# The last half of a down projection summed on 128 partitions of 64 columns instead of 32 partitions of 256

## The chip, the cores and the metric

The kernel runs on one core of one Trainium2 chip. The metric is the device time of one execution in microseconds (us); three runs of the kernel before took 438.18, 437.98 and 438.04, median 438.04. The core has five engines that run their own instruction streams and wait for each other by semaphores: PE (TensorE, the matrix array, with its weight loads shown apart as PEld), DVE (VectorE), ACT (ScalarE), POOL (GpSimd) and SP (SyncE, which here only issues transfers). Sixteen transfer engines move data between memory (HBM) and the on-chip SBUF. TensorE writes into PSUM, from which VectorE and ScalarE read. SBUF and PSUM have 128 partitions; a matmul loads a stationary operand ("weights" of the array, up to 128 columns wide) and streams a moving operand past it, column by column; the stationary columns become the partitions of the result.

## What is computed

One decoding step of a transformer block for 8 sequences of one token each, width 1024:

```
mod = (silu(c) @ w_mod) in six parts: sa, ca, ga, sb, cb, gb
h = layernorm(x) * (1 + ca) + sa
x = x + ga * attention(h)        # 32 query heads on 4 cached heads, 8192 cached keys and values each
h = layernorm(x) * (1 + cb) + sb
g = h @ W_gate ; u = h @ W_up    # 1024 -> 3584
x = x + gb * ((relu(g) * u) @ W_down)   # 3584 -> 1024
```

Inputs and outputs are bfloat16. The change is in the last line: the product with W_down, the gate gb, the residual, and the store of the result, which is 8 rows of 1024.

## The kernel before

All weights and both caches (185 MB) are read once, by transfers that SP issues in the order of the list `stream` into one large SBUF tile, `ring`, of five slots. A transfer waits for the matmuls that used what lay in its place before. Instructions are written out in program order for each engine; a small graph (`_Graph`, lines 36 to 232) turns data dependences into semaphore waits. No planner moves anything.

The first part makes mod, the normalised input and the queries. The middle loop goes over 16 pairs of cached heads and is followed by the output projection. The last part, which the change touches, goes like this:

- Lines 691 to 697: the attention result becomes `x1T`, the residual stream with the width on partitions (128 x 8 x 8), and is normalised to `h2T`.
- Lines 700 to 709: 128 matmuls for gate and up, in eight steps of k. After step 3 stand two calls of `to_rows` (line 540). `to_rows` brings gb and `x1T` from the width-on-partitions form into the form in which the result will be made: VectorE multiplies the source by the mask `part` into the tile `wide` (f32, eight blocks of 128 columns), TensorE multiplies each block of `wide` by the mask `rest`, and VectorE copies the result out of PSUM into `gbR` or `x1R`. In this kernel the form is 32 partitions of interest (partition 32 q + b, for quarter q of the width and sequence b) of 256 columns each.
- Lines 710 to 716: relu and product, `hmR`; seven transposes and a copy make `hmT`, the stationary operand of the down projection: 128 partitions, 7 x 4 blocks of 8 columns (one column for each sequence).
- Lines 719 to 723: the first half of W_down, block ("wd", 0), 28 matmuls of 8 weight columns by 512, into four strips of partitions of the PSUM bank `Y`. Line 724 copies it to `yR`.
- Lines 725 and 726, the fold: two f32 matmuls with the selection matrix `fold` add up the four strips of `yR` and lay the sum out as 256 columns on the 32 partitions, in the PSUM tile `W`. In the profile an f32 matmul shows as two records.
- Lines 727 to 736: the second half of W_down, blocks ("wd", 1) to ("wd", 4), 56 matmuls of 8 weight columns by 256, four at a time side by side: quarter q of the width into the strip of partitions that begins at 32 q. They add to the fold's result in PSUM.
- Lines 737 and 738: VectorE multiplies by `gbR` into `fR` and adds `x1R` into `outR`.
- Lines 739 to 741: four stores, one for each quarter, of eight pieces of 512 bytes; two issued on SP, two on ACT. Line 755 waits for all four.

The masks and cleared tiles (`part`, `rest`, `wide`, `fold`, lines 460 to 466) are made at the start, on VectorE.

In the profile the helper lines stand for all operations: line 422 is every matmul, 426 every transpose, 430 every VectorE operation, 433 every ScalarE operation, 747 every load, 87 every other transfer.

Of the kernel before, what the change touches and what calls it, by code (L numbers as in the profile page):

```python
# [7 lines left out]
ALU = mybir.AluOpType  # L8
AX = mybir.AxisListType
# [225 lines left out]
def bass_adaLN_cond__gqa_block_cached__glu_gated_reglu__decode_kernel(  # L235
# [14 lines left out]
    B, _, D = A_x.shape  # L250
# [7 lines left out]
    KD = D // 128  # L258
# [7 lines left out]
    g = _Graph()  # L266
    f32, bf16 = dt.float32, dt.bfloat16

    with ExitStack() as es:
        E = es.enter_context  # L270

        def sb(name, shape, dtype):
            return E(nc.sbuf_tensor(name, shape, dtype))
# [5 lines left out]
        identf = sb("identf", [128, 128], f32)  # L279
# [8 lines left out]
        yR = sb("yR", [128, 512], f32)  # L288
# [12 lines left out]
        ov = sb("ov", [128, 256], f32)  # L301
# [6 lines left out]
        diag = sb("diag", [128, 2, 128], bf16)  # L308
        blk = sb("blk", [128, 8, 16], f32)
        pick = sb("pick", [128, 2, B], f32)  # L310
        fold = sb("fold", [128, 2, 128], f32)
        og = sb("og", [128, 2, 16], f32)
        spare = sb("spare", [128, 2, 16], bf16)
        ot = sb("ot", [128, 2, 16, B], bf16)
        hmT = sb("hmT", [128, 7, 4, B], bf16)
        part = sb("part", [128, 4], f32)
        rest = sb("rest", [128, 32], f32)
        wide = sb("wide", [128, KD, 128], f32)
        gbR = sb("gbR", [128, 256], f32)
        x1R = sb("x1R", [128, 256], f32)  # L320
        outR = sb("outR", [128, 256], bf16)
# [5 lines left out]
        fR = ov[:, 0:256]  # L327
# [4 lines left out]
        osem = E(nc.semaphore("d_o"))  # L332
# [46 lines left out]
        wd = B_W_down.rearrange("(q p i) n -> p q i n", q=4, i=7)  # L379
# [13 lines left out]
        for key, at, cols, src, shape, slot in stream:  # L393
# [3 lines left out]
            t = ring[:, lo:hi]  # L397
# [6 lines left out]
            o = _Op("sp", None, 0)  # L404
# [7 lines left out]
        def pe(fn, reads=(), writes=(), block=None, deps=()):  # L412
            deps = list(deps)
            if block is not None:
                deps.append(loads[block])
            o = g.op("pe", fn, reads, writes, deps)
            if block is not None:
                users[block] = o
            return o

        def mm(out_, lhsT, rhs, start, stop, reads, writes, block=None, deps=()):
            return pe(lambda e: e.matmul(out_, lhsT, rhs, start=start, stop=stop, skip_group_check=True),  # L422
                      reads, writes, block, deps)

        def tr(out_, in_, ident, reads, writes, block=None):
            return pe(lambda e: e.matmul(out_, in_, ident, start=True, stop=True, is_transpose=True),  # L426
                      reads, writes, block)

        def dve(name, *args, reads=(), writes=(), **kw):
            return g.op("dve", lambda e: getattr(e, name)(*args, **kw), reads, writes)  # L430
# [29 lines left out]
        dve("tensor_reduce", part[:], identf[:].rearrange("p (q x) -> p q x", q=4), AX.X, ALU.add, reads=["identf"], writes=["part"])  # L460
        dve("tensor_reduce", rest[:], identf[:].rearrange("p (q x) -> p x q", q=4), AX.X, ALU.add, reads=["identf"], writes=["rest"])
        dve("memset", wide[:], 0.0, writes=["wide"])
        dve("memset", fold[:], 0.0, writes=["fold"])
        for i in range(2):
            dve("tensor_reduce", fold[:, i].rearrange("p (h s r) -> p h s r", h=2, s=2)[:, :, i, :],
                identf[:].rearrange("p (a h r) -> p h r a", a=2, h=2), AX.X, ALU.add, reads=["identf", "fold"], writes=["fold"])
        dve("tensor_reduce", pick[:], identf[:].rearrange("p (s h x) -> p h x s", s=2, h=2)[:, :, 0:B, :], AX.X, ALU.add, reads=["identf"], writes=["pick"])
        for i in (0, 1, 2, 3, 7):
            dve("memset", bank(i), 0.0, writes=[pB[i]])
# [37 lines left out]
        for k in range(KD):  # L507
            w = place[("mod", k // 4)][:, k % 4, :]
# [5 lines left out]
        t = PS[:, 4, :]  # L514
# [19 lines left out]
        for j in range(2):  # L534
            dve("tensor_copy", qT[:, :, 16 * j:16 * (j + 1)].rearrange("p b (q i) -> p i q b", i=4),
                TB(0)[:, 0:512].rearrange("p (i q x) -> p i q x", i=4, q=4)[:, :, :, B * j:B * (j + 1)],
                reads=[pT[0], ("KT", 2)], writes=["qT", ("KT", 2)])


        def to_rows(dst, dkey, src, skey):  # L540
            dve("tensor_tensor", out=wide.rearrange("p k (q x) -> p k q x", q=4)[:, :, :, 0:B], in0=src[:, :, None, :].to_broadcast([128, KD, 4, B]),
                in1=part[:, None, :, None].to_broadcast([128, KD, 4, B]), op=ALU.mult, reads=[skey, "part"], writes=["wide"])
            for k in range(KD):
                mm(W[:, 32 * k:32 * (k + 1)], wide[:, k, :], rest[:], True, True, ["wide", "rest"], [pW])
            dve("tensor_copy", dst.rearrange("p (x k) -> p k x", k=8), W[:, 0:256].rearrange("p (k x) -> p k x", k=8), reads=[pW], writes=[dkey])


        turn = [0]
# [90 lines left out]
        Y, pY = bank(0), pB[0]  # L639
# [73 lines left out]

        for i in range(7):
            tr(TB(0)[:, 128 * i:128 * (i + 1)], hmR[:, i:896:7], identb[:], [("KT", 2), "identb"], [pT[0]])
        dve("tensor_copy", hmT[:], TB(0)[:, 0:896].rearrange("p (i q x) -> p i q x", i=7, q=4)[:, :, :, 0:B], reads=[pT[0]], writes=["hmT"])


        for t in range(14):
            w = place[("wd", 0)][:, t // 7, t % 7, :]  # L720
            for h in range(2):
                at = 64 * (t % 2) + 32 * h
                mm(Y[at:at + B, :], hmT[:, t % 7, t // 7, :], w[:, 512 * h:512 * (h + 1)], t < 2, t >= 12, ["hmT"], [pY], ("wd", 0))
        dve("tensor_copy", yR[:], Y, reads=[pY], writes=["yR"])
        for i in range(2):
            mm(W[:, 0:256], fold[:, i], yR[:, 256 * i:256 * (i + 1)], i == 0, False, ["yR", "fold"], [pW])
        for c_ in (2, 3):
            for i in range(7):
                if c_ == 2:
                    key, w = ("wd", 1), place[("wd", 1)][:, i, :]  # L730
                else:
                    u = 2 + (i >= 4) + (i >= 6)
                    key, w = ("wd", u), place[("wd", u)][:, i - (0, 4, 6)[u - 2], :]
                for q in range(4):
                    mm(W[32 * q:32 * q + B, 0:256], hmT[:, i, c_, :], w[:, 256 * q:256 * (q + 1)], False, c_ == 3 and i == 6,
                       ["hmT"], [pW], key)
# [18 lines left out]
        nc.sync.wait_ge(osem, 64)  # L755


# [26 lines left out]
```

## Time and profile before

| what | us |
|---|---|
| median of three runs | 438.04 |
| span of the profiled execution, first to last instruction | 436.3 |
| TensorE busy | 307.2 (70%) |
| ScalarE busy | 208.4 (48%) |
| VectorE busy | 180.0 (41%) |
| GpSimd busy | 12.6 (3%) |
| bytes moved, mean rate | 185.81 MB, 426 GB/s |

The record holds no separate time of the profiled execution; its span is 1.7 us under the median of the runs. The page divides the span into 40 slices of 10.9 us and gives a digit for each (9 is 90% busy or more); PEclk is the share of its full clock that TensorE was granted. The chain of work that ended last is followed back from the last instruction. The timeline gives the start, the duration, the engine, the line, the operation, what it writes and reads, its shapes, how many were merged, and in brackets how long the engine had been idle and what ended that. A table by windows gives, for each stretch, its length, the busy time and count for PE, PEld, DVE, ACT and POOL, then the granted clock, the share of the transfer engines and GB/s.

### The profile page before, as it was taken

What the parts mean: (1) busy time and instruction counts of PE and PEld (TensorE: products, weight loads), DVE (VectorE), ACT (ScalarE), POOL (GpSimd) and SP (SyncE); (2) the same over time, 40 slices, a digit from 0 to 9 for tenths busy, and PEclk for the clock granted to TensorE, in tenths of its full rate; (3) what the DMA queues carried; (4) which work ended last, traced back from release to release, by engine and by line L of the source; (5) the groups of instructions that cost most, each with busy time, mean ns of one, the idle gap of its engine ahead of it and who ended that gap; (6) DMA issues with size and microseconds to landing.
All of it is one profiled execution on the core that took longest, in us unless ns stands there. A gap on an engine that the chain in (4) does not pass through costs nothing.

```text
span 436.3 us, 10723 instructions
## 1 busy us (share of the span) xinstructions
PE 307.2 (70%) x4575; PEld 200.1 (46%) x4575; DVE 180.0 (41%) x384; ACT 208.4 (48%) x246; POOL 12.6 (3%) x52
## 2 busy tenths in 40 slices
PE   0104257989878888787888888777888878755356
PEld 0101025656555555554555555555555555432323
DVE  3600036456363644536264553536364453331111
ACT  2200005676756747675664757576575747400000
POOL 6000000000000000000000000000000000000000
PEclk9999599999999999999999999999999999885766
DMA  8999999999999999999999999999999999999996
GB/s 339 433 433 446 431 431 432 434 431 431 433 436 433 436 433 436 433 436 433 433 436 433 436 436 433 433 436 436 433 436 433 433 433 433 420 422 439 430 419 251
DMA packets 7003, 185.81 MB, mean 426 GB/s; under 512 B 800, under 2 KB 832, under 8 KB 1104
## 3 DMA queue, kind: packets, MB, share of 16 engines
q1 hardware_dynamic: 6928, 185.61, 98.8%
q8 instruction: 9, 0.15, 0.1%
q10 hardware_dynamic: 64, 0.04, 0.0%
q14 instruction: 2, 0.02, 0.0%
HBM read 185.63 MB, written 0.02 MB: 426 GB/s over the span
## 4 chain that ended last, share of the span: by engine, by line
DMA 54%; PE 23%; DVE 9%; issue 8%; ACT 5%; SPq 0%; DVEq 0%; ACTq 0%; POOL 0%
DMA ring<-in_A_k_cache_dram 34%; PE PS L422 13%; DMA ring<-in_w_mod_dram 11%; PE PS L426 11%; DMA ring<-in_B_W_down_dram 8%; ACT P L433 3%; DVE KT L430 2%; ACT KT L433 2%; DVE tm L430 2%; DVE ov L430 1%; DVE nm L430 1%; DVE mp L430 1%; DVE rl L430 0%; DVE nb L430 0%; DVE qT L430 0%
## 5 line engine op out<-in xcount | busy, mean ns | idle before, releaser
L433 ACT ACTIVATE KT<-PS 128x1024 bf16<-128x1024 bf16 (+1 forms) x130 | 131.9, 1016 | 164.2 <-PE PS L426 137.7
L426 PE MATMUL PS<-identb,ring 128*128 128x128 bf16 x2048 | 152.8, 220 | 22.0 <-DMA ring<-in_A_k_cache_dram 20.3
L430 DVE COPY KT<-PS 128x1024 bf16<-128x1024 bf16 (+1 forms) x129 | 88.9, 689 | 164.2 <-PE PS L426 129.1
L426 PEld LDWEIGHTS PS<-identb,ring 128*128 128x128 bf16 x2048 | 117.0, 98 | 61.3 <-issue 36.9
L422 PE MATMUL PS<-KT,Z 128*32 128x512 bf16 x516 | 51.9, 389 | 0.1
L422 PE MATMUL PS<-ring,pt 128*32 128x256 bf16 x1088 | 49.8, 274 | 0.6 <-DVE pt L430 0.6
L433 ACT ACTIVATE P<-PS,nb 64x1024 bf16<-64x1024 f32 x34 | 37.7, 1108 | 6.2 <-DVE nb L430 4.2
L426 PE MATMUL PS<-identb,P 128*128 128x128 bf16 x272 | 21.1, 221 | 20.2 <-ACT P L433 14.5
L422 PEld LDWEIGHTS PS<-ring,pt 128*32 128x32 bf16 x1088 | 24.5, 95 | 12.8 <-issue 0.8
L422 PE MATMUL PS<-ring,siluT 128*24 128x512 bf16 x96 | 8.6, 531 | 27.6 <-DMA ring<-in_w_mod_dram 27.6
L426 PEld LDWEIGHTS PS<-identb,P 128*128 128x128 bf16 x272 | 15.5, 98 | 26.5 <-DVE KT L430 17.2
L433 ACT ACTIVATE pt<-PS 64x512 bf16<-64x512 bf16 x34 | 20.1, 591 | 13.5 <-PE PS L426 13.3
L430 DVE COPY pt<-PS 64x512 bf16<-64x512 bf16 x34 | 14.4, 422 | 17.7 <-PE PS L426 17.2
L430 DVE TENSOR_REDUCE mp<-PS 128x1 f32<-128x1024 f32 x17 | 20.7, 1215 | 0.0
L422 PEld LDWEIGHTS PS<-KT,Z 128*32 128x32 bf16 x516 | 13.3, 92 | 13.8 <-ACT KT L433 0.5
L422 PE MATMUL PS<-ring,h2T 128*8 128x512 bf16 (+1 forms) x128 | 10.5, 494 | 11.7 <-DMA ring<-in_B_W_up_dram 9.8
L433 ACT ACT_TABLE_LOAD x11 | 14.1, 1283 | 8.4 <-DMA KT<-in_A_x_dram 8.3
L422 PEld LDWEIGHTS PS<-ring,siluT 128*24 128x24 bf16 x96 | 2.9, 120 | 33.0 <-DMA ring<-in_w_mod_dram 28.3
L426 PE MATMUL PS<-identb,KT 128*128 128x128 bf16 (+1 forms) x19 | 1.7, 217 | 18.4 <-DVE KT L430 18.4
L637 POOL CAST ot<-og 128x16 bf16<-128x16 f32 x16 | 4.1, 254 | 291.0 <-DVE og L430 291.0
L422 PE MATMUL PS<-od,selo 128*128 128x128 f32 x36 | 8.8, 326 | 5.1 <-DVE od L430 5.1
L422 PEld LDWEIGHTS PS<-ring,h2T 128*8 128x8 bf16 x128 | 3.5, 109 | 18.0 <-DMA ring<-in_B_W_up_dram 11.1
(99 smaller groups left out, 163.3 us busy)
## 6 DMA issues: line engine op xcount, KB each, us to landing
ring<-in_A_k_cache_dram SPq DMA_DIRECT2D x16, 4096.0 KB, 21.6
ring<-in_A_v_cache_dram SPq DMA_DIRECT2D x16, 4096.0 KB, 30.5
ring<-in_w_mod_dram SPq DMA_DIRECT2D x2, 6144.0 KB, 42.5
ring<-in_A_wq_dram SPq DMA_DIRECT2D x2, 4096.0 KB, 16.9
ring<-in_A_wo_dram SPq DMA_DIRECT2D x2, 4096.0 KB, 29.5
ring<-in_B_W_gate_dram SPq DMA_DIRECT2D x2, 3584.0 KB, 24.9
ring<-in_B_W_up_dram SPq DMA_DIRECT2D x2, 3584.0 KB, 31.0
ring<-in_B_W_down_dram SPq DMA_DIRECT2D x1, 3584.0 KB, 36.2
```

The source lines that it names most:

```text
L422: return pe(lambda e: e.matmul(out_, lhsT, rhs, start=start, stop=stop, skip_group_check=True), reads, writes, block, deps)
L426: return pe(lambda e: e.matmul(out_, in_, ident, start=True, stop=True, is_transpose=True), reads, writes, block)
L430: return g.op("dve", lambda e: getattr(e, name)(*args, **kw), reads, writes)
L433: return g.op("act", lambda e: e.activation(*args, **kw), reads, writes)
L637: pool(lambda e: e.tensor_copy(dst, og[:, n % 2]), reads=[("og", n % 2)], writes=[("ot", n // B)])
```

## The change

The second half of the down projection, the fold, the gate, the residual and the output take another form: partition 32 q + 8 z + b, for quarter q, a quarter z of that quarter, and sequence b, with 64 columns each, so that all 128 partitions hold results.

- `hmT` becomes 7 x 4 blocks of 56 columns, cleared at the start, with the eight columns of values at 24 to 32. A slice of 32 columns that begins at 24 - 8 z holds the values at columns 8 z to 8 z + 8 and zeros beside them, so a matmul with it adds to one group of eight partitions of a strip and adds zero to the others.
- Each of the 56 matmuls becomes four (z = 0 to 3), with 32 weight columns and 64 streamed columns: 224.
- The fold becomes eight f32 matmuls of 64 columns, with 128-column slices of a `fold` tile of 184 columns.
- `part`, `rest`, `gbR`, `x1R`, `outR` and `fR` change shape. `to_rows` writes all of `wide` each time, so `wide` is no longer cleared at the start.
- Four stores become one, on SP, of 128 pieces of 128 bytes.

```diff
-        fold = sb("fold", [128, 2, 128], f32)
+        fold = sb("fold", [128, 184], f32)
-        hmT = sb("hmT", [128, 7, 4, B], bf16)
-        part = sb("part", [128, 4], f32)
-        rest = sb("rest", [128, 32], f32)
+        hmT = sb("hmT", [128, 7, 4, 56], bf16)
+        part = sb("part", [128, 16], f32)
+        rest = sb("rest", [128, 8], f32)
...
-        dve("memset", wide[:], 0.0, writes=["wide"])
         dve("memset", fold[:], 0.0, writes=["fold"])
-        for i in range(2):
-            dve("tensor_reduce", fold[:, i].rearrange("p (h s r) -> p h s r", h=2, s=2)[:, :, i, :],
-                identf[:].rearrange("p (a h r) -> p h r a", a=2, h=2), AX.X, ALU.add, reads=["identf", "fold"], writes=["fold"])
+        dve("tensor_reduce", fold[:, 56:184].rearrange("p (h r) -> p h r", h=2)[:, :, 0:B],
+            identf[:].rearrange("p (a h r) -> p h r a", a=2, h=2)[:, :, 0:B, :], AX.X, ALU.add, reads=["identf", "fold"], writes=["fold"])
+        dve("memset", hmT[:], 0.0, writes=["hmT"])
...
         def to_rows(dst, dkey, src, skey):
-            dve("tensor_tensor", out=wide.rearrange("p k (q x) -> p k q x", q=4)[:, :, :, 0:B], in0=src[:, :, None, :].to_broadcast([128, KD, 4, B]),
-                in1=part[:, None, :, None].to_broadcast([128, KD, 4, B]), op=ALU.mult, reads=[skey, "part"], writes=["wide"])
+            dve("tensor_tensor", out=wide.rearrange("p k (g x) -> p k g x", g=16), in0=src[:, :, None, :].to_broadcast([128, KD, 16, B]),
+                in1=part[:, None, :, None].to_broadcast([128, KD, 16, B]), op=ALU.mult, reads=[skey, "part"], writes=["wide"])
             for k in range(KD):
-                mm(W[:, 32 * k:32 * (k + 1)], wide[:, k, :], rest[:], True, True, ["wide", "rest"], [pW])
-            dve("tensor_copy", dst.rearrange("p (x k) -> p k x", k=8), W[:, 0:256].rearrange("p (k x) -> p k x", k=8), reads=[pW], writes=[dkey])
+                mm(W[:, 8 * k:8 * (k + 1)], wide[:, k, :], rest[:], True, True, ["wide", "rest"], [pW])
+            dve("tensor_copy", dst.rearrange("p (x k) -> p k x", k=8), W[:, 0:64].rearrange("p (k x) -> p k x", k=8), reads=[pW], writes=[dkey])
...
-        dve("tensor_copy", hmT[:], TB(0)[:, 0:896].rearrange("p (i q x) -> p i q x", i=7, q=4)[:, :, :, 0:B], reads=[pT[0]], writes=["hmT"])
+        dve("tensor_copy", hmT[:, :, :, 24:32], TB(0)[:, 0:896].rearrange("p (i q x) -> p i q x", i=7, q=4)[:, :, :, 0:B], reads=[pT[0]], writes=["hmT"])
...
-        for i in range(2):
-            mm(W[:, 0:256], fold[:, i], yR[:, 256 * i:256 * (i + 1)], i == 0, False, ["yR", "fold"], [pW])
+        for u in range(8):
+            mm(W[:, 0:64], fold[:, 56 - 8 * u:184 - 8 * u], yR[:, 64 * u:64 * (u + 1)], u == 0, False, ["yR", "fold"], [pW])
...
-                for q in range(4):
-                    mm(W[32 * q:32 * q + B, 0:256], hmT[:, i, c_, :], w[:, 256 * q:256 * (q + 1)], False, c_ == 3 and i == 6,
-                       ["hmT"], [pW], key)
-        dve("tensor_tensor", out=fR, in0=W[:, 0:256], in1=gbR[:], op=ALU.mult, reads=[pW, "gbR"], writes=["ov"])
+                for z in range(4):
+                    for q in range(4):
+                        at = 256 * q + 64 * z
+                        mm(W[32 * q:32 * (q + 1), 0:64], hmT[:, i, c_, 24 - 8 * z:56 - 8 * z], w[:, at:at + 64], False, c_ == 3 and i == 6 and z == 3,
+                           ["hmT"], [pW], key)
+        dve("tensor_tensor", out=fR, in0=W[:, 0:64], in1=gbR[:], op=ALU.mult, reads=[pW, "gbR"], writes=["ov"])
         dve("tensor_tensor", out=outR[:], in0=fR, in1=x1R[:], op=ALU.add, reads=["ov", "x1R"], writes=["outR"])
-        for q in range(4):
-            g.dma("sp" if q % 2 == 0 else "act", out.rearrange("b o d -> (b o) d")[:, 256 * q:256 * (q + 1)], outR[32 * q:32 * q + B, :],
-                  osem, 16 * (q + 1), reads=["outR"])
+        g.dma("sp", out.rearrange("b o (g c) -> g (b o) c", g=16), outR[:], osem, 16, reads=["outR"])
...
-        nc.sync.wait_ge(osem, 64)
+        nc.sync.wait_ge(osem, 16)
```

More of the change, by code (lines that the diff above doesn't have):

```diff
@@ L314, in bass_adaLN_cond__gqa_block_cached__glu_gated_reglu__decode_kernel @@
         ot = sb("ot", [128, 2, 16, B], bf16)
-        hmT = sb("hmT", [128, 7, 4, B], bf16)
-        part = sb("part", [128, 4], f32)
-        rest = sb("rest", [128, 32], f32)
+        hmT = sb("hmT", [128, 7, 4, 56], bf16)
+        part = sb("part", [128, 16], f32)
+        rest = sb("rest", [128, 8], f32)
         wide = sb("wide", [128, KD, 128], f32)
-        gbR = sb("gbR", [128, 256], f32)
-        x1R = sb("x1R", [128, 256], f32)
-        outR = sb("outR", [128, 256], bf16)
+        gbR = sb("gbR", [128, 64], f32)
+        x1R = sb("x1R", [128, 64], f32)
+        outR = sb("outR", [128, 64], bf16)
         row, sig = KT[0:2 * B, 0, :], KT[0:2 * B, 1, :]
@@ L326, in bass_adaLN_cond__gqa_block_cached__glu_gated_reglu__decode_kernel @@
         hmR = KT[:, 2, :]
-        fR = ov[:, 0:256]
+        fR = ov[:, 0:64]
         PS = E(nc.psum_tensor("PS", [128, 8, 512], f32))
@@ L459, in bass_adaLN_cond__gqa_block_cached__glu_gated_reglu__decode_kernel @@
         spread(identf[:].rearrange("p (y k) -> p k y", k=8), 8, blk, "blk")
-        dve("tensor_reduce", part[:], identf[:].rearrange("p (q x) -> p q x", q=4), AX.X, ALU.add, reads=["identf"], writes=["part"])
-        dve("tensor_reduce", rest[:], identf[:].rearrange("p (q x) -> p x q", q=4), AX.X, ALU.add, reads=["identf"], writes=["rest"])
-        dve("memset", wide[:], 0.0, writes=["wide"])
+        dve("tensor_reduce", part[:], identf[:].rearrange("p (g x) -> p g x", g=16), AX.X, ALU.add, reads=["identf"], writes=["part"])
+        dve("tensor_reduce", rest[:], identf[:].rearrange("p (g x) -> p x g", g=16), AX.X, ALU.add, reads=["identf"], writes=["rest"])
         dve("memset", fold[:], 0.0, writes=["fold"])
-        for i in range(2):
-            dve("tensor_reduce", fold[:, i].rearrange("p (h s r) -> p h s r", h=2, s=2)[:, :, i, :],
-                identf[:].rearrange("p (a h r) -> p h r a", a=2, h=2), AX.X, ALU.add, reads=["identf", "fold"], writes=["fold"])
+        dve("tensor_reduce", fold[:, 56:184].rearrange("p (h r) -> p h r", h=2)[:, :, 0:B],
+            identf[:].rearrange("p (a h r) -> p h r a", a=2, h=2)[:, :, 0:B, :], AX.X, ALU.add, reads=["identf", "fold"], writes=["fold"])
+        dve("memset", hmT[:], 0.0, writes=["hmT"])
         dve("tensor_reduce", pick[:], identf[:].rearrange("p (s h x) -> p h x s", s=2, h=2)[:, :, 0:B, :], AX.X, ALU.add, reads=["identf"], writes=["pick"])
@@ L722, in bass_adaLN_cond__gqa_block_cached__glu_gated_reglu__decode_kernel @@
                 at = 64 * (t % 2) + 32 * h
-                mm(Y[at:at + B, :], hmT[:, t % 7, t // 7, :], w[:, 512 * h:512 * (h + 1)], t < 2, t >= 12, ["hmT"], [pY], ("wd", 0))
+                mm(Y[at:at + B, :], hmT[:, t % 7, t // 7, 24:32], w[:, 512 * h:512 * (h + 1)], t < 2, t >= 12, ["hmT"], [pY], ("wd", 0))
         dve("tensor_copy", yR[:], Y, reads=[pY], writes=["yR"])
-        for i in range(2):
-            mm(W[:, 0:256], fold[:, i], yR[:, 256 * i:256 * (i + 1)], i == 0, False, ["yR", "fold"], [pW])
+        for u in range(8):
+            mm(W[:, 0:64], fold[:, 56 - 8 * u:184 - 8 * u], yR[:, 64 * u:64 * (u + 1)], u == 0, False, ["yR", "fold"], [pW])
         for c_ in (2, 3):
```

## The prediction

> **What bounds the kernel now.** I read the page's slices first, then the chain of work that ended last, then the last 10 us instruction by instruction, and then the transfers' landings.
>
> ```profile
> span 436.3 us, 10723 instructions
> PEclk9999599999999999999999999999999999885766
> DMA  8999999999999999999999999999999999999996
> ```
>
> The transfer engines are nine tenths busy or more in all slices but the first and the last: the kernel is a stream from memory with work hung behind it. The change touches only what stands after the last bytes, so the question is which wait ends last there. The chain, in order of time:
>
> ```profile
> 388.23 36.21 DMA ring<-in_B_W_down_dram
> 424.44 0.04 issue
> 424.48 3.19 PE PS L422 x28
> 427.67 0.02 issue
> 427.69 0.70 DVE yR L430
> 428.40 0.04 issue
> 428.44 5.04 PE PS L422 x45
> 433.48 0.02 issue
> 433.50 0.43 DVE ov L430
> 433.94 0.02 issue
> 433.96 0.42 DVE outR L430
> ```
>
> From 424.48 no transfer stands on the chain: TensorE, VectorE, TensorE, VectorE, store. The timeline of the same stretch and the last four transfers (KB, us from issue to landing):
>
> ```profile
> 403.18 1.76 SPq L747 DMA_DIRECT2D ring<-in_B_W_down_dram  x4
> ...
> 428.44 2.07 PE L422 MATMUL PS<-yR,fold 128*128 128x256 f32 x4 [0.80 <-DVE yR L430]
> ...
> 430.44 3.00 PE L422 MATMUL PS<-ring,hmT 128*8 128x256 bf16 x56
> 433.05 0.09 PEld L422 LDWEIGHTS PS<-ring,hmT 128*8 128x8 bf16 x4 [0.17 <-DMA ring<-in_B_W_down_dram]
> ...
> 434.41 0.71 SPq L87 DMA_DIRECT2D out_dram<-outR  x2
> ```
> ```profile
> ring<-in_B_W_down_dram SPq DMA_DIRECT2D x1, 1792.0 KB, 25.5
> ring<-in_B_W_down_dram SPq DMA_DIRECT2D x1, 1024.0 KB, 27.6
> ring<-in_B_W_down_dram SPq DMA_DIRECT2D x1, 512.0 KB, 28.3
> ring<-in_B_W_down_dram SPq DMA_DIRECT2D x1, 256.0 KB, 28.5
> ```
>
> The four issues lie some 0.45 us apart from 403.18, so the blocks land near 428.7, 431.2, 432.4 and 433.0. The last weight load waited only 0.17 us for the last block: TensorE reaches the last block just as it lands. So TensorE has 0.17 us to spare in this tail, and everything beyond that lengthens the kernel one for one.
>
> **The change, part by part.** The sum is made against this execution's span, 436.3 us; the median of the runs, 438.04, lies 1.74 above it, and I add that unchanged.
>
> *The fold of the first half.* Two f32 products of 256 columns (four records) become eight of 64 columns (sixteen records), each with its own load of 128 f32 weight columns. The streamed columns stay 512 (2 x 256, 8 x 64), but the loads go from four to sixteen. The same load elsewhere: sixteen records of `to_rows`, and then a table by windows (PE busy and count first, the clock third from the end) in which the first two rows hold two records each of the layernorm's f32 matmul of 64 columns, the third the sixteen, the fourth the fold:
>
> ```profile
> 403.44 1.97 PE L422 MATMUL PS<-rest,wide 128*128 128x32 f32 x16
> ```
> ```profile
> 391.50:392.10 0.60, 0.43 (x2) 0.30 (x2) 0.07 (x2) 0.00 (x0) 0.00 (x0) 1.00 1.11 478
> 392.80:393.60 0.80, 0.69 (x2) 0.50 (x2) 0.02 (x2) 0.00 (x0) 0.00 (x0) 0.50 1.08 466
> 403.40:405.50 2.10, 2.01 (x20) 1.86 (x16) 0.05 (x1) 0.00 (x0) 0.00 (x0) 1.00 1.01 437
> 428.40:430.40 2.00, 1.96 (x4) 1.17 (x4) 0.00 (x0) 0.00 (x0) 0.00 (x0) 0.50 0.98 414
> ```
>
> At the full clock sixteen such records took 1.97 us and two took 0.43, so one more costs (1.97 - 0.43) / 14 = 0.110 us; 32 or 64 columns hardly differ beside the load. The fold runs at clock 0.50 (last row). There a pair took 0.69, and one more costs 0.110 if the load did not slow at all, 0.220 if it halves with the clock. The fold would then take 0.69 + 14 x 0.110 = 2.2 to 0.69 + 14 x 0.220 = 3.8 us against 2.07. I take 0.220, because the pair itself went from 0.43 to 0.69: the load does slow. That is +1.7 us (bounds +0.1 and +1.7), and TensorE's next matmul starts at 430.44 + 1.7 = 432.15.
>
> *The second half.* 56 matmuls of 8 weight columns by 256 become 224 of 32 by 64, still four side by side in four column strips. Fifty-six took 3.00 us at clock 0.50: 14 rows of four, 0.214 each. A row of four by 64 is a quarter, 0.0535, if streaming stays the limit; 56 rows again give 3.0 us. Side-by-side strips with 32 weight columns do stream at full rate where 256 columns follow each load:
>
> ```profile
> 379.90:381.90 2.00, 1.93 (x64) 1.68 (x64) 0.00 (x0) 1.96 (x3) 0.00 (x0) 1.00 0.99 426
> ```
>
> Sixty-four in 1.93 us at the full clock, 0.121 per row of four, 0.030 per 64 columns. No row shows 64 columns behind a load of 32, so: lower bound 0.030 per row (full clock), upper bound four times 0.0535 (the four do not overlap). I take 0.0535, the nearest form at this clock. By 432.15 two blocks are in SBUF; the third lands at 432.4 and the last at 433.0, well before rows 45 and 53, which need them: no load is waited for any more. The 56th row starts at 432.15 + 55 x 0.0535 = 435.1; before, the last row's drain and the hand-over took about 0.33 (433.17, which is 430.44 plus 13 x 0.21, to 433.50). VectorE starts at 435.4 instead of 433.50: **+1.9** for both matmul parts.
>
> *Gate and residual.* Two operations of 256 columns become two of 64. Rows of that form:
>
> ```profile
> 391.06 0.22 DVE L430 TENSOR_TENSOR x1T<-PS,modT 128x64 f32<-128x64 f32 x1 [2.13 <-PE PS L422]
> 391.31 0.22 DVE L430 TENSOR_TENSOR x1T<-x1T,xT 128x64 f32<-128x64 f32 x1
> ```
>
> 0.22 each against 0.42 to 0.43: **-0.4**, all of it on the chain.
>
> *The store.* Four issues on two queues become one on SP. Before, the first issue started at 434.41 and the span ended at 436.3; the second on SP was worth about half of its 0.71, so -0.35 if the last landing simply moves up. But 128 pieces of 128 bytes replace 32 of 512, eight per transfer engine instead of one or two, which no row shows; as bound above I double the wait after the last issue:
>
> ```profile
> SPq L755 <- DMA out_dram<-outR: 1.1, 1, 1.1
> ```
>
> That gives -0.35 to +1.1. I take **0**. ACT loses its two issues, and behind SP's single one stands only the closing wait, now for one landing instead of four.
>
> *Row forms of gate and residual, and set-up.* Both spreading products now write all 1024 f32 columns of `wide` instead of 256, at most four times the 0.42 of the first row here; the copies out of PSUM shrink.
>
> ```profile
> 395.20 0.42 DVE L430 TENSOR_TENSOR wide<-modT,part 128x256 f32<-128x256 f32 x1
> ...
> 415.96 4.54 PE L422 MATMUL PS<-ring,h2T 128*8 128x512 bf16 x56 [7.13 <-DMA ring<-in_B_W_up_dram]
> ```
> ```profile
> PE PS L422 <- DMA ring<-in_w_mod_dram: 27.6, 2, 17.7
> ```
>
> The first has from 395.20 to the sixteen records at 403.44, the second pushes its own sixteen back by 1.3 us at most, under the 7.13 us that TensorE then waits for W_up; without that cover, +1.3. The last four issues hang on matmuls ahead of this step and do not move. The copy into `hmT` strides now; it is done before the first w_down block lands at 424.44, and would cost some 0.1 without that. In set-up one clearing and one reduction go and another clearing comes, on VectorE; TensorE waits 27.6 us for w_mod after it, so 0.
>
> Sum: +1.9 - 0.4 + 0 = **+1.5**, span 437.8, time **439.5**.
>
> **The rivals.**
>
> *The clock opens under the tail (0.27).* Everything after 432.15 then streams at the full clock from about 433.1, where it rose before:
>
> ```profile
> 426.30:429.70 3.40, 2.60 (x19) 1.22 (x8) 0.69 (x1) 0.00 (x0) 0.00 (x0) 0.50 0.96 405
> 429.70:433.10 3.40, 3.40 (x54) 1.77 (x57) 0.00 (x0) 0.00 (x0) 0.00 (x0) 0.50 0.67 270
> 433.20:436.30 3.10, 0.24 (x8) 0.00 (x0) 0.85 (x2) 0.00 (x0) 0.00 (x0) 1.00 0.03 5
> ```
>
> A stretch busy throughout was followed by clock 1.00, one with 2.60 of 3.40 busy was not. 18 rows by 433.1, 38 at 0.030: VectorE starts near 434.55, +1.05 - 0.4 = +0.65, 438.7. Against it: until 432.15 the array would stream half of the time and load for the rest, which may count as less than busy; so I keep the half clock as likelier. [...]
>
> *The loads show (0.13).* If a load of 32 columns cannot hide under only 64, each row of four pays it. The f32 load of 128 columns is 0.110 at the full clock (above), 32 columns of it 0.027; half the bytes and half the clock leave that as an estimate. 56 x 0.027 = 1.5: 441.0. For it: no row streams so little behind such a load. Against it: in the row of 379.90 the loads hide wholly, and 0.027 is less than the 0.0535 of streaming.
>
> *The four strips do not overlap when short (0.10).* Half of the overlap lost makes 224 x 0.027 = 6.0 instead of 3.0: 442.5; all of it lost, 448. For it: no row is that short. Against it: both longer forms overlap fully. [...]
>
> *Not slower (0.13).* If the clock has opened before the fold, at 427 to 428, sixteen records take 1.97 and 52 rows 1.6: TensorE is done with the first three blocks at 432.0, waits for the last at 433.0 as now, and only the -0.4 remains, with the store's -0.35 at best: 437.3 to 437.6. It decides once fold and 52 rows together stay under 433.0 - 428.44 = 4.6 us; my forecast has 6.5. The stretch 426.30 to 429.70 at 0.50 speaks against it.
>
> **How the numbers follow.** My forecast has 0.37, the rivals 0.27, 0.13, 0.10 and 0.13. What a measurement of this kernel can tell from no change is about 0.2%, 0.9 us: 437.2 to 438.9. Slower: my case, the loads, the overlap and a quarter of the clock rival, 0.67. Same: the rest of the clock rival and most of the last, 0.29. Faster needs more than the two VectorE operations and the whole second issue together, 0.04. The range leaves out the lost overlap and most of the not-slower case: 438.0 to 441.6; my case with the store's bounds alone is 439.1 to 440.6.
>
> **What would show it.** Fold: sixteen records over 3.8 us, ending near 432.2, at clock 0.50. Tail: 224 matmuls in about 3.2 us with no wait for the last block; VectorE from 435.4 in two operations of 0.22; one store ending 1.9 us after its issue. I am wrong if the fold takes 2 us, if the clock rises at 433, if the 224 take over 4 us, or if VectorE still starts at 433.5.

## The result: 440.35 us against 438.04, slower by half a per cent

The changed kernel took 440.35 us (median of five runs, 440.01 to 440.66), the kernel before 438.04 (five runs, 437.87 to 438.18): a ratio of 1.0047, 95% interval 1.0033 to 1.0061. The forecast was 439.5 in 438.0 to 441.6, slower. The profiled execution took 440.66 us with a span of 439.0, so 1.7 us lie around the span, as before. The page's first line, its row for the reads of instructions (how many, MB, share of the transfer engines), and its row for the store:

```profile
span 439.0 us, 11079 instructions
q8 instruction: 10, 0.16, 0.1%
out_dram<-outR SPq DMA_DIRECT2D x1, 16.0 KB, 1.9
```

The span grew by 2.7 us, where the forecast's sum had 1.5. The end of the chain of work after the change (start, us, what):

```profile
427.74 0.02 issue
427.76 0.70 DVE yR L430
428.46 0.04 issue
428.50 5.79 PE PS L422 x156
434.29 1.46 issue
435.75 0.71 PE PS L422 x60
436.46 0.02 issue
436.49 0.23 DVE ov L430
436.72 0.02 issue
436.75 0.22 DVE outR L430
```

The chain before had one unbroken piece of TensorE here. Now a line "issue" of 1.46 us cuts it: TensorE stands still there and waits for nothing that the profile shows. The timeline of the same stretch:

```profile
428.50 3.68 PE L422 MATMUL PS<-yR,fold 128*128 128x64 f32 x16 [0.80 <-DVE yR L430]
432.11 2.18 PE L422 MATMUL PS<-ring,hmT 128*32 128x64 bf16 x164
435.75 0.66 PE L422 MATMUL PS<-ring,hmT 128*32 128x64 bf16 x60 [1.46 <-issue]
435.75 0.55 PEld L422 LDWEIGHTS PS<-ring,hmT 128*32 128x32 bf16 x60 [1.57 <-issue]
437.00 0.64 SPq L87 DMA_DIRECT2D out_dram<-outR  x1
```

The gap falls inside the 224 matmuls, after 164 of them, with all weights there (the last block of w_down is complete at 433.03), and matmuls and weight loads stop together. The clock, in a table by windows (PE busy, PEld busy, then the other engines; the clock third from the end):

```profile
428.40:432.10 3.70, 3.60 (x16) 3.49 (x16) 0.05 (x1) 0.00 (x0) 0.00 (x0) 0.50 0.89 368
432.10:434.30 2.20, 2.19 (x165) 2.07 (x164) 0.00 (x0) 0.00 (x0) 0.00 (x0) 0.59 0.15 52
434.30:435.70 1.40, 0.00 (x0) 0.00 (x0) 0.00 (x0) 0.00 (x0) 0.00 (x0) 1.00 0.00 0
```

The clock stood at one half for the fold and for most of the 164 matmuls, and opened at about 433.9 (a mean of 0.59 over 2.2 us is 0.4 us at the full clock).

Where the 2.7 us come from, by these rows against those of before: TensorE's first matmul after the fold 430.44 to 432.11, +1.67; from there to VectorE's start 3.06 before and 4.38 now, of which 1.46 is the gap and the rest, 2.92, is 0.14 shorter; from VectorE's start to the store 0.91 before and 0.51 now, -0.40; store to the end 1.9 and 2.0, +0.1.

### The profile page after: what moved, and what is told of

Its sections match the earlier page's. It is cut to its first block, busy times and chain, and to the rows that moved or that the text cites. A ratio compares the mean times of both kernels' runs of the same rounds, so it can differ in the third digit from the quotient of the medians.

```text
span 439.0 us, 11079 instructions
## 1 busy us (share of the span) xinstructions
PE 311.1 (71%) x4755; PEld 205.5 (47%) x4755; DVE 179.7 (41%) x383; ACT 208.4 (47%) x246; POOL 12.6 (3%) x52
## 4 chain that ended last, share of the span: by engine, by line
DMA 54%; PE 23%; DVE 9%; issue 8%; ACT 5%; SPq 0%; DVEq 0%; ACTq 0%; POOL 0%
DMA ring<-in_A_k_cache_dram 34%; PE PS L422 12%; DMA ring<-in_w_mod_dram 11%; PE PS L426 11%; DMA ring<-in_B_W_down_dram 9%; ACT P L433 3%; DVE KT L430 2%; ACT KT L433 2%; DVE tm L430 2%; DVE ov L430 1%; DVE nm L430 1%; DVE mp L430 1%; DVE rl L430 0%; DVE nb L430 0%; DVE qT L430 0%
## 5 line engine op out<-in xcount | busy, mean ns | idle before, releaser
L422 PE MATMUL PS<-ring,h2T 128*8 128x512 bf16 (+1 forms) x128 | 11.6, 534 | 10.0 <-DMA ring<-in_B_W_up_dram 8.1
```

## The experiments

Two theories on the gap. *Instructions*: each matmul shows as two instructions, a load and a product (4755 of each on the page after the change). If TensorE gets them in blocks of 256, 128 matmuls of this form are done before the next block is there. (A crossing, below, is the moment at which TensorE goes over from one block to the next; its time is worked out from the count of matmuls.) *Something in the data or in PSUM* at that place of the sum, or the clock's change at 433.9: then the gap stays with the 164th matmul, or with the clock, whatever stands ahead of it. Instructions put in front of the tail move the block ends. They were meant to move nothing else; in the traces the clock is in another phase too (e2, e5), and one landing is late (e1, e2).

### The gap follows the count of instructions

e1_shift112, e2_shift256 and e5_shift40 are the changed kernel with 56, 128 and 20 tiny matmuls, whose results are never read, among the gate and up projections, where TensorE waits for weights anyway (28, 64 or 10 in each of two steps):

```diff
             for b0, nm_ in ((0, "gate"), (2, "up")):
+                if b0 == 2 and k in (0, 4):
+                    for _ in range(28):
+                        mm(bank(5)[0:B, 0:1], h2T[:, 0, :], identb[:, 0:1], True, True, ["h2T", "identb"], [pB[5]])
```

> The changed kernel with 56 tiny matmuls (8 weight columns by 1, result never read), 28 each in two places where TensorE idles for W_up: 112 more instructions on TensorE (each matmul is a weight load and a product) ahead of the tail, nothing else. Theory, code: the gap of 1.46 us after the 164th of the 224 matmuls is TensorE waiting for its next 16 KB block of instructions; blocks end every 256 instructions, so 112 more ahead of the tail put the block ends 232 and 488 instructions before the program's end instead of 120 and 376, and the last block is then asked for during the first half of w_down, some 5 us before it is needed. The gap goes, VectorE starts near 435.0, the time is 438.9 (438.7 to 439.2). Rival, place: the gap belongs to the 164th matmul, the clock's rise or the last block of w_down; it stays and the time is 440.3.

> The same with 128 tiny matmuls, 64 in each place: 256 more instructions, one whole block. Theory, code: the block ends fall where they were, so the gap is back after the 164th of 224 with 1.4 to 1.6 us and the time is 440.3 (440.0 to 440.7). Rival, warmth: if the tiny matmuls of the run with 112 took the gap away because they kept TensorE busy, twice as many take it away too and the time is 438.9.

> The same with 20 tiny matmuls, 10 in each place: 40 more instructions. Theory, code: the gap moves 20 matmuls ahead, to after the 144th of 224, with about the same length; time 440.3 (439.8 to 440.7), as what follows the gap runs at the full clock either way. Rival, place: it stays after the 164th.

Measured: e1 439.02 us (438.83 to 439.51, ten runs; ratio to before 1.0021, 1.0012 to 1.0031), e2 442.13 (440.80 to 442.49, four runs; 1.0095, 1.0078 to 1.0111), e5 440.21 (439.74 to 440.42, four runs; 1.0045, 1.0028 to 1.0062). The times of e1 and e5 and the places of all gaps are as expected. The gaps of e2 (2.19 us) and e5 (3.16 us) are longer than expected, and e2's time is outside its expected range. The timeline and a window of e1:

```profile
428.45 3.68 PE L422 MATMUL PS<-yR,fold 128*128 128x64 f32 x16 [0.80 <-DVE yR L430]
432.06 3.18 PE L422 MATMUL PS<-ring,hmT 128*32 128x64 bf16 x224
435.29 0.23 DVE L430 TENSOR_TENSOR ov<-PS,gbR 128x64 f32<-128x64 f32 x1 [6.89 <-PE PS L422]
```
```profile
432.06:435.24 3.18, 3.17 (x225) 3.01 (x224) 0.00 (x0) 0.00 (x0) 0.00 (x0) 0.50 0.14 48
```

The timeline of e2, whose profiled execution, 440.80 us, is the shortest of its four:

```profile
425.96 3.11 PE L422 MATMUL PS<-ring,hmT 128*8 128x512 bf16 x28 [3.92 <-DMA ring<-in_B_W_down_dram]
431.80 1.52 PE L422 MATMUL PS<-ring,hmT 128*32 128x64 bf16 x164
435.51 0.86 PE L422 MATMUL PS<-ring,hmT 128*32 128x64 bf16 x60 [2.19 <-issue]
```

The timeline of e5:

```profile
428.37 2.00 PE L422 MATMUL PS<-yR,fold 128*128 128x64 f32 x16 [0.81 <-DVE yR L430]
430.30 1.35 PE L422 MATMUL PS<-ring,hmT 128*32 128x64 bf16 x144
434.81 1.26 PE L422 MATMUL PS<-ring,hmT 128*32 128x64 bf16 x80 [3.16 <-issue]
```

With 40 instructions ahead the gap comes 20 matmuls earlier, after 144. With 256 it is back after 164, the same place. With 112 a block ends 108 matmuls into the tail and the one before it ends ahead of the fold; between the two, the fold's 3.6 us give the next block time, and there is no gap. So the gap is a wait for instructions, and it comes back after 256 of them. The trace's own records of 16 KB instruction reads agree: in the changed kernel one begins at 433.31, and in each of the five gaps of the changed kernel, e2, e5 and e4 (below) TensorE goes on 2.2 to 2.7 us after such a read began.

The gap isn't the clock's: in e5 the clock was open for the fold (sixteen records in 2.00 us) and up to the gap, TensorE reached the block's end 2.6 us sooner (431.65 against 434.29), and yet VectorE started only 0.37 us sooner. Of the 2.6 us the longer gap, 3.16 us, took back 1.7. Another 0.6 went behind the gap, where 80 matmuls were left in place of 60 and, by their pace, the clock was at one half again (1.26 us against 0.66; 15.8 ns each, where e1 at 0.50 has 14.2 and the changed kernel at 1.00 behind its gap 11). In e2 the whole tail starts 1.5 us late, because one completion of the first block of w_down was late (see below). Its three other executions took 1.3 to 1.7 us longer than the profiled one; why isn't shown.

Without the fold the tail is longer, and the spacing shows (e4_nofold64, the changed kernel with all four quarters of the product in the narrow form):

```diff
-        for t in range(14):
-            ...
-        dve("tensor_copy", yR[:], Y, reads=[pY], writes=["yR"])
-        for u in range(8):
-            mm(W[:, 0:64], fold[:, 56 - 8 * u:184 - 8 * u], yR[:, 64 * u:64 * (u + 1)], u == 0, False, ["yR", "fold"], [pW])
-        for c_ in (2, 3):
+        for c_ in range(4):
             for i in range(7):
```

> The changed kernel without copy and fold: the first half of w_down also in the 64-column form, 448 matmuls of 32 by 64 (896 instructions) in all. Theory, code: a block of 256 instructions comes 3.5 us after it is asked for and 256 instructions of this form run in 1.7 us at half clock, so TensorE has two gaps of 1.4 to 2 us (about 427 and 430.5) and works on its last block of code from about 432.2; with one landing late by 1.5, VectorE starts near 434.9: 439.0 (438.6 to 440.0). Rival: the gaps do not come, and what is left is the late landing or nothing: 437.6 to 439.1.

It took 441.26 us (440.87 to 442.58, four runs; 1.0082, 1.0065 to 1.0099). The expectation missed: it had two gaps, but of 1.4 to 2 us each. The timeline of its shortest execution, 440.87 us:

```profile
424.60 1.89 PE L422 MATMUL PS<-ring,hmT 128*32 128x64 bf16 x208 [2.22 <-DMA ring<-in_B_W_down_dram]
431.01 1.90 PE L422 MATMUL PS<-ring,hmT 128*32 128x64 bf16 x128 [4.51 <-issue]
435.01 1.69 PE L422 MATMUL PS<-ring,hmT 128*32 128x64 bf16 x112 [2.11 <-issue]
```

Exactly 128 matmuls, 256 instructions, stand between two gaps. They run for 1.90 us and the next block comes 4.00 us after the last. In the changed kernel the crossing before the gap is 36 matmuls into the tail (164 less 128), at about 432.6, and the next block is there at 435.75, 3.2 us later. Ahead of e4's first gap the crossing is 80 matmuls into the tail (208 less 128), at about 425.3, and the next block is there only at 431.01, 5.7 us later; its read begins at 428.73, with the weights still streaming.

A turn of the middle loop shows 1035 instructions of TensorE, some four times 256, and seven turns, from 100.9 to 370.2 us in the changed kernel, ran without one instruction read. So, by this trace, TensorE can keep about four blocks or more, and what the tail lacked was not room but the next block in time: each read in the tail began only after a crossing (at 433.31 after 432.6 in the changed kernel, at 428.73 after 425.3 in e4).

### The fold by itself depends on the clock's phase

e3_fold16 is the kernel before with its fold cut into eight products of 64 columns, sixteen records:

```diff
-            mm(W[:, 0:256], fold[:, i], yR[:, 256 * i:256 * (i + 1)], i == 0, False, ["yR", "fold"], [pW])
+            for u in range(4):
+                mm(W[:, 64 * u:64 * (u + 1)], fold[:, i], yR[:, 256 * i + 64 * u:256 * i + 64 * (u + 1)], i == 0 and u == 0, False, ["yR", "fold"], [pW])
```

> The kernel before with its fold alone cut: two f32 products of 256 columns become eight of 64 (sixteen records, each with its load of 128 columns), laid out as before; all else as before. Theory: at clock 0.50 sixteen records take 3.7 us instead of 2.07 and TensorE has 0.17 us to spare, so VectorE starts 1.5 to 1.6 us later and the time is 439.6 (439.3 to 439.8). Rival: the loads hide under the wait for the last blocks of w_down and the time stays at 438.0 to 438.3.

It took 439.28 us (437.93 to 440.00, ten runs; 1.0020, 1.0005 to 1.0036), just under the expected range. The spread is wide, and the profiled execution, 438.15 us, is one of the shorter ones. Its timeline:

```profile
424.63 1.69 PE L422 MATMUL PS<-ring,hmT 128*8 128x512 bf16 x28 [2.14 <-DMA ring<-in_B_W_down_dram]
427.11 2.00 PE L422 MATMUL PS<-yR,fold 128*128 128x64 f32 x16 [0.80 <-DVE yR L430]
433.21 0.39 PE L422 MATMUL PS<-ring,hmT 128*8 128x256 bf16 x4 [0.25 <-DMA ring<-in_B_W_down_dram]
```

Here the sixteen records took 2.00 us, about the 1.97 of the sixteen of `to_rows` at clock 1.00 before, so the clock was open in the tail; TensorE then waited for each block (0.25 us for the last) and finished with the last bytes. So sixteen records take 3.68 us at half clock (the changed kernel, e1) and 2.00 with the clock open, and the second is no loss here. That the longer runs are those with the closed clock is likely but was not seen in a tail, since only one execution is profiled: the three runs under 438.2 us had a mean granted clock of 0.943 to 0.946 over their span, the seven others 0.934 to 0.941.

### A late landing, and what goes with it

The traces show sixteen completions for each block of weights, and the matmuls that need it start behind the last of them (in e10 it stands at 434.45, the matmuls at 434.49). In e1 one of the sixteen completions of the second block came 1.6 us after the others, and the last block was complete at 434.44 instead of 433.0 (e1's last matmuls come later still and don't wait for it). Four kernels looked into this. e8_before_shift48 and e10_before_shift112 are the kernel before with 24 and 56 of the tiny matmuls, in the same place as above; e6_nofold256 and e7_nofold128 are the kernel before without the fold, in 256 columns and in 128 columns (16 partitions of each strip).

> The kernel before with 24 tiny matmuls (8 weight columns by 1, never read), 12 in each of the two places where TensorE idles for W_up: 48 more TensorE instructions, all work of the tail as before. Theory, fetch: a block of instructions is fetched through one of the sixteen transfer engines. In the runs with 112 and 256 more instructions the ninth fetch came at 428.3 and 419.8, while the weights still streamed, and from then on exactly one of the sixteen landings of each block was 1.5 us late; in the kernel before the ninth fetch comes at 432.7, behind the data. With 48 more it comes near 427.5 to 428.5, one landing of the last block is 1.4 to 1.5 us late, TensorE waits for it, and the time is 439.5 (439.3 to 439.7). Rival: 24 tiny matmuls under a wait cost nothing, 438.0 to 438.2.

> The kernel before with 56 tiny matmuls ahead of the projections (112 instructions of TensorE more, as many as in e1_shift112; their results are never read). Its second half is 56 matmuls of 256 columns, which never waited for instructions, so instruction supply by itself should cost nothing: 438.1 by it alone. Theory that a fetch of instructions pushes back the one of the 16 transfer engines that carries it, by about 1.4 us, and that the weights are never complete before the slowest of the sixteen: the fetch falls at about 428 us as in e1, the last block of w_down is complete at 434.4 in place of 433.0, VectorE starts at 434.9 and the time is 439.5 (439.2 to 439.8). Rival, that e1's late landing came from the changed kernel itself or from chance: 438.1 (437.9 to 438.4), last landing at 433.0.

> The kernel before without copy and fold of the first half: the first half of w_down goes straight into the 256-column form too (56 matmuls instead of 28, 48 more instructions in all on TensorE). Theory: TensorE has work to spare, so the end hangs on the last landing alone; the ninth fetch comes near 428, one landing is 1.5 us late, 439.5 (439.2 to 439.7). Rival: without the late landing it equals the kernel before, 438.0, or is 0.1 faster.

> No fold, and the form half way: 16 partitions of each strip by 128 columns (224 matmuls of 16 by 128 in all), gate, residual and output on 128 columns, four stores of sixteen pieces. Theory: TensorE keeps up, VectorE's two operations take 0.29 each instead of 0.42 (-0.25), the ninth fetch comes near 427 and one landing is 1.5 us late: 439.2 (438.9 to 439.5). Rival: the fetch falls on a transfer engine that has time to spare; then 437.8, faster than the kernel before.

The core of the edits of e6 and e7, the second of which also reshapes the masks, `gbR`, `x1R`, `outR` and the stores:

```diff
-        for c_ in (2, 3):
+        for c_ in range(4):
...
+                for z in range(2):
+                    for q in range(4):
+                        at = 256 * q + 128 * z
+                        mm(W[32 * q:32 * q + 16, 0:128], hmT[:, i, c_, 24 - 8 * z:40 - 8 * z], w[:, at:at + 128], c_ == 0 and i == 0 and z == 0, c_ == 3 and i == 6 and z == 1,
+                           ["hmT"], [pW], key)
```

Measured: e8 438.01 us (437.80 to 439.41, ten runs; 1.0007, 0.9997 to 1.0016), e10 439.43 (439.26 to 439.48, six runs; 1.0029, 1.0017 to 1.0041), e6 439.44 (439.31 to 440.30, seven runs; 1.0033, 1.0022 to 1.0045), e7 440.51 (440.00 to 441.30, four runs; 1.0051, 1.0034 to 1.0068). e10 met its expectation and e6 its number; e8 and e7 missed theirs. From the chain of e8:

```profile
433.12 0.04 issue
433.17 0.31 PE PS L422 x4
433.51 0.43 DVE ov L430
```

From the timeline of e10, and from its chain:

```profile
433.88 0.39 PE L422 MATMUL PS<-ring,hmT 128*8 128x256 bf16 x8 [0.61 <-DMA ring<-in_B_W_down_dram]
434.49 0.39 PE L422 MATMUL PS<-ring,hmT 128*8 128x256 bf16 x4 [0.22 <-DMA ring<-in_B_W_down_dram]
```
```profile
405.08 29.37 DMA ring<-in_B_W_down_dram
434.45 0.04 issue
434.93 0.43 DVE ov L430
```

The two kernels differ only in the count of tiny matmuls. e10's last block is complete at 434.45 and e8's at 433.12, and the spans, 437.7 and 436.3 us, differ by about as much; in both TensorE waits for that block. The trace's records of transfers, 16 KB instruction reads after 400 us and the last two of the sixteen completions of the last block of w_down:

```
kernel    instruction reads begin at            15th and 16th completion
before    419.34  432.66                        432.99  433.01
after     420.00  433.31  436.93                433.02  433.03
e8        411.90  432.66                        433.06  433.12
e10       410.80  428.32                        432.98  434.45
e1        410.90  428.32  434.18                433.04  434.44
e4        419.54  428.73  432.53  436.05        433.10  434.55
e7        420.23  429.42  440.31                433.26  434.32
e2        404.42  419.82  432.80  436.55        432.95  434.43
e6        421.83  432.72                        433.59  434.99
```

In all four kernels that had a read between the last blocks (428.3 to 429.4), one completion was 1.1 to 1.6 us late from then on, and the lag stayed to the end. Reads from 432.5 on came too late to touch a block; e3, e5 and e9, with no read between 420.1 and 432.4, were on time. Reads at 404 to 422 mostly did nothing; in e2 the lag begins in the block after 419.82. In e6 it is there, at about 1.4 us, from the cache block that lands at 113 us to the end; there the other fifteen are 0.6 us late too, and both together make the time of its profiled execution (439.98 us, VectorE at 435.48). The theory of e8 and e10, that such a read holds up the one transfer engine that carries it, fits all of these, but it isn't shown: which engine carries a read the trace doesn't tell, so why most of the earlier reads cost nothing stays open. The lag took no part in the profiled execution of the changed kernel, where all sixteen are on time.

### The change taken half way

e9_fold128: 64 partitions of 128 columns, with the fold, four stores. The core of it:

```diff
-            mm(W[:, 0:256], fold[:, i], yR[:, 256 * i:256 * (i + 1)], i == 0, False, ["yR", "fold"], [pW])
+        for u in range(4):
+            at = 32 * (u // 2) + 8 * (u % 2)
+            mm(W[:, 0:128], fold[:, 40 - at:168 - at], yR[:, 128 * u:128 * (u + 1)], u == 0, False, ["yR", "fold"], [pW])
...
+            g.dma("sp" if q % 2 == 0 else "act", out.rearrange("b o (q z c) -> q z (b o) c", q=4, z=2)[q], outR[32 * q:32 * q + 16, :],
```

> The change taken half way: the same sum as 128 columns on each of 64 partitions, the fold as eight float32 products of 128 columns, the second half as 112 matmuls, four stores of sixteen pieces. TensorE has 120 instructions more than in the kernel before, so no end of 256 instructions falls where fewer than 256 are in reach: by the theory that instruction supply made the changed kernel slow there is no idle time without a cause between the fold and the end. Fold 2.1 us at half clock (four of 256 columns took 2.07), 28 rows of four at 0.106 us (the same rows without the fold), VectorE at 433.5, two steps of 0.29 in place of 0.42: 437.9 (437.7 to 438.3), the same as before or 0.1% faster. Rival, that the narrow form costs by itself, half as much as the changed kernel did: 439.2 (438.8 to 439.6), with the fold longer than 2.5 us or idle time of TensorE inside the second half.

It took 438.94 us (438.80 to 440.52, eight runs; 1.0034, 1.0021 to 1.0046), in the range of the rival, but not by its mechanism. Five runs lie at 438.80 to 438.94 and three at 440.43 to 440.52; the profiled one, 438.81, is of the five, and what the three lost isn't shown. Its timeline:

```profile
427.29 2.07 PE L422 MATMUL PS<-yR,fold 128*128 128x128 f32 x8 [0.79 <-DVE yR L430]
433.21 0.29 PE L422 MATMUL PS<-ring,hmT 128*16 128x128 bf16 x8 [0.23 <-DMA ring<-in_B_W_down_dram]
433.55 0.29 DVE L430 TENSOR_TENSOR ov<-PS,gbR 128x128 f32<-128x128 f32 x1 [6.32 <-PE PS L422]
434.20 1.44 SPq L87 DMA_DIRECT2D out_dram<-outR  x2
```

There is no gap; fold and VectorE are as expected, and the second VectorE step ends 0.2 us sooner than before. All of it is lost in the store: two issues on a queue take 1.44 us where they took 0.71, and the span ends 2.9 us after the first issue (434.20 to 437.1) against 1.9 before. e7, which has the same stores, shows 1.45, and with its late landing that makes its span of 438.4 us. In two of e7's four runs 2.5 to 2.9 us lie around the span in place of 1.7; in the profiled one of them an instruction read begins at 440.31, behind the span's end. No version here beats the kernel before; one with this sum and the old store cost would gain 0.2 us, less than can be told, and wasn't tried.

## Why the prediction was right, and where a term was missing

- **What bounds the tail.** Right at half clock: the chain before had 0.17 us to spare, and what was added to TensorE's tail came out at the end. With the clock open TensorE waits for the last blocks instead (e3).
- **The fold, +1.7.** Right to 0.04 us: sixteen records in 3.68 us at clock 0.50, the next matmul at 432.11 against 432.15. The choice of 0.220 per record at half clock holds; e3 and e5 show the other bound, 2.00 us, when the clock is open.
- **The second half, 0.0535 per row of four.** Right as a rate: 224 in 3.18 us in e1, VectorE at 435.29 against 435.4. The loads of 32 columns hide under products of 64 (in e1 3.01 us of loads lie within 3.17 of products), and the four short strips overlap (14.2 ns a matmul in e1 at clock 0.50; 164 in 1.52 us in e2, 9 ns each), so the rivals that the loads show and that the strips do not overlap fall.
- **What failed: the step "no load is waited for any more. The 56th row starts at 432.15 + 55 x 0.0535 = 435.1".** It lets 56 rows run without a break once the weights are there. It counted matmuls by their streaming and weights by their landing and put the supply of the instructions themselves at nothing, without a reason. The missing term is the wait for the next block: 1.46 us, VectorE at 436.49 instead of 435.4. From the first to the last, the 224 matmuls took 4.3 us (432.11 to 436.41), beyond the 4 us that the forecast named as a sign of being wrong.
- **The number.** That 440.35 lies in the range, even in the 439.1 to 440.6 of the forecast's own case, is partly luck: the upper part of that stretch stood for a slow store, which did not come, and the missing term filled it.
- **The clock rival (0.27).** It came true by a small part: the clock rose at 433.9, not 433.1, which took some 0.3 us off the tail (2.92 against e1's 3.23). The forecast's doubt, that the fold may count as less than busy, fits e1. A window of the changed kernel, after which the clock rose, and then the like window of e1, after which it did not (in these traces the granted clock changes only in steps of 3.41 us, which gives the windows):

```profile
430.40:433.80 3.40, 3.40 (x137) 3.28 (x140) 0.00 (x0) 0.00 (x0) 0.00 (x0) 0.50 0.49 192
```
```profile
430.10:433.50 3.40, 3.40 (x122) 3.28 (x124) 0.00 (x0) 0.00 (x0) 0.00 (x0) 0.50 0.55 220
```

  Both are busy throughout; the fold has 1.7 us of the first and 1.9 of the second. After the first the clock was 1.00 (433.9 to 434.3), after the second it was still 0.50 (433.6 to 435.2). What decides between the two was not tested. Had the clock opened earlier, the wait at the block's end would have taken most of the gain, as in e5; so this rival's 438.7 was out of reach.
- **Not slower (0.13).** Its condition, an open clock at the fold, occurred in e5's profiled execution, and that still took 440.32 us; the same missing term.
- **Gate and residual, -0.4.** Right: two steps of 0.22 to 0.23, -0.40 to the store.
- **The store, 0 between -0.35 and +1.1.** Right: 1.9 us from issue to landing, the closing part 0.1 us longer. 128 pieces of 128 bytes in one issue cost within 0.1 us what 32 of 512 in four did.
- **`to_rows` and set-up at nothing.** Right; the spreading product takes 1.21 us, and TensorE still waits 4.33 us for W_up behind it, though the sixteen records that follow it took 3.58 us at half clock against 1.97 before:

```profile
405.95 1.21 DVE L430 TENSOR_TENSOR wide<-x1T,part 128x1024 f32<-128x1024 f32 x1
415.97 0.92 PE L422 MATMUL PS<-ring,h2T 128*8 128x512 bf16 x8 [4.33 <-DMA ring<-in_B_W_up_dram]
```

e1 has every term of the sum and no gap: 439.02, and its profiled execution, with the clock at half through the tail, has a span of 437.7 us against the sum's 437.8. The wait for the block of instructions makes up the rest to 440.35.

## What to carry to other kernels

Count instructions as well as work: cutting each matmul into four makes four times the instructions, and here 256 of them had to last 3.2 to 5.7 us or TensorE waited for the next block. Where a stretch of many short instructions stands on the last chain, see where the block ends fall in it. The sign is an "issue" line on an engine whose data are all there; the test is to move it by a few dummy instructions. A kernel whose end hangs on the last byte can also move by 1.3 us when instructions are added far ahead of its tail (e10, 439.43 against 438.14), so a difference of 0.3% between two versions needs the landings compared before it is put down to the edit.

## What the runs showed of the hardware that was not expected

- TensorE's waits for instructions stand 256 instructions apart (128 matmuls between the two gaps of e4); 256 more ahead of the tail left the gap after the 164th matmul (e2), 40 more moved it 20 matmuls forward (e5). In this tail the next block was usable 3.2 us (the changed kernel) to 4.4 us (e5) after the crossing before it, 4.0 us from block to block in e4, and 5.7 us in e4 while the weights streamed; its 16 KB read takes 0.9 to 1.4 us of that in the trace.
- TensorE ran a loop of some 1035 instructions, about four such blocks, for seven turns without an instruction read, and still did not have the next block ready in time in the straight code of the tail.
- After such a read between the last blocks, while the weights streamed, one of the sixteen completions of every later block was 1.1 to 1.6 us late (e1, e4, e7, e10).
- In e1 the clock stayed at one half after a window of 3.4 us in which TensorE was busy throughout; 1.9 of the 3.4 us were the f32 fold with its 128-column loads. In the changed kernel, with 1.7, it opened.
- Two stores on a queue took 1.44 us to issue with 16 pieces of 256 bytes each (e9) against 0.71 with 8 of 512, while one of 128 pieces of 128 bytes took 0.64. What in the form of the transfer makes this was not tested.
